# A fused chunk attention and wave MLP on one core: the written-out order of steps is replaced by another

## The chip, the core and the metric

The kernel runs on one core of a Trainium2 chip. The core has a matrix engine (PE, TensorE; its weight loads are listed apart as PEld), a vector engine (DVE), a scalar engine (ACT), GpSimd (POOL), and a sync engine (SP) that only issues transfers. Each engine executes its own list of instructions in order, and waits at an instruction for what another engine or a transfer has to bring. The metric is device time in microseconds (us); below, all times without a unit are us.

## The reference

Eight batches of 576 tokens with 8 heads of 64. Attention is local to chunks of 64 tokens; its output x (576 x 512 per batch) goes through a "wave" mixer over tokens and a channel mixer:

```python
scores = scale * np.matmul(q_c, k_c.transpose(0, 1, 2, 4, 3))   # 9 chunks of 64 x 64 per head
attn = np.exp(scores) / sum
out = np.matmul(attn, v_c)                                      # = x
theta = x @ w_theta
zr, zi = x * np.cos(theta), x * np.sin(theta)
y = np.einsum('ts,bsd->btd', w_tok_r, zr) + np.einsum('ts,bsd->btd', w_tok_i, zi)
u = x + y
return u + np.maximum(u @ w_ch, 0.0)
```

## The kernel before

Batches go in pairs p = 0 to 3. The 1152 tokens of a pair are nine row tiles of 128 (j = 0 to 8): tiles 0 to 3 of the first batch, 4 to 7 of the second, and tile 8 (M) with the last 64 tokens of both. Attention works on five groups of a pair: A (tiles 0, 1), B (2, 3), C (4, 5), D (6, 7) and M (8). Tensors are fp16 in SBUF, sums fp32 in PSUM, whose eight banks and all SBUF buffers are handed out by hand.

The whole program is a table, `ORDER`, of some 610 steps. Its order is the order in which each engine gets its instructions; no scheduler moves them. A step reads `kind.at.slot`: `S.0B.2` is the kind S on pair 0, group B, with bank 2. Numbers after `at` are banks or buffers; so a new order also hands out banks and buffers anew. An instruction that reuses one waits for its last reader.

The kinds, in the order in which a group passes them:

- `qk` loads q and k of a group (POOL's queue), `v` its v, `lw` a row tile of the two token matrices (`lw.03` is tile 3), `lp` w_theta, `lc` w_ch. `qk0.0A` and `qk1.0A` are the first two loads: heads 0 to 3 and 4 to 7 of group 0A, in fp32 by SP and ACT; `cy0` and `cv1` cast them on ACT and DVE.
- `T` (or `Tq`, `Tk`, `T0`, `T1`) transposes q and k in 32 x 32 blocks on DVE; `S` the score products on PE; `E` the exp on ACT; `V0`, `V1` the products with v for four heads each; `N0`, `N1` the division by the sum (a reciprocal and a product on DVE), which writes x.
- `X` turns x on PE, and `xa`, `xv` copy it out by ACT or DVE; `xd` does both by a transposing DMA from SP. `H` is the product with w_theta (four products of 512 columns a tile), `G` cos and sin on ACT, `Z` the two products on DVE that give zr and zi.
- `TW` turns a token tile (ten PE transposes), `twv` or `twa` copies it out by DVE or ACT. `Y` (or `Ya`, `Yb`, `Ym` for the shares of A, B and M, or of C, D and M) is the token product of an output tile, `A` the addition to x on DVE. For most of pairs 2 and 3 the token product is done on 2 x 2 blocks with fewer products: `sw`, `za`, `zb`, `zm` are the sums on DVE, `K` the products, `B` the additions.
- `U` turns u with `ua` or `uv` as copies, `ud` by DMA; `W` is the product with w_ch, `R` relu and addition on DVE, `st`, `sa`, `sg` the store, issued by SP, ACT or POOL.
- `dm.n.b` issues n products of zeros of full width into bank b. They serve no output.

ACT holds one table of functions at a time, exp or cos and sin; `table` loads the other when a step needs it.

Of the kernel before, what the change touches and what calls it, by code (L numbers as in the profile page):

```python
# [11 lines left out]
AF = mybir.ActivationFunctionType  # L12
ALU = mybir.AluOpType
# [5 lines left out]
Tk.0B v.0M v.0B Tq.0M.5 lw.03.2 S.0B.2 T1.0A E0.0A.0 V0.0A.0 Tk.0M S1.0A.4 E1.0A S.0M.6 lp.00 E.0M.1  # L19
V0.0M.7 N0.0A V1.0M.6 qk.0C.4 N1.0M V1.0A.4 dm.2.0 E.0B.2 lw.01.5 V1.0B.2 V0.0B.0 N1.0A X.0A.4  # L20
qk.1M.1 lw.02.3 N1.0B N0.0B xa.0A.1 X.0B.5 TW.03.3 v.0C N0.0M X.0M.7 xv.0B.2 H1.0A.5 G1.0A.0 H1.0B.0
G1.0B.3 xv.0M.4 Tq.0C.2 Z1.0A H0.0A.7 qk.0D.0 lw.00.6 G0.0A.1 v.0D twv.03 Z0.0A H.0M.5 H0.0B.4
G.0M.4 TW.01.6 G0.0B.1 Ya.03.3 Tk.0C S.0C.0 Z1.0B twv.01 v.1M E.0C.3 Z0.0B Ya.01.6 Yb.01 TW.02.4
twa.02 Z.0M Ym.01 T.1M.2 A.01 Yb.03 V0.0C.0 Ym.03 V1.0C.4 Tq.0D.1 S.1M.6 E.1M.4 Ya.02.7 Yb.02 Ym.02
N1.0C Tk.0D S.0D.4 N0.0C A.03 TW.00.0 qk.1B.2 A.02 X.0C.3 lw.04.0 E.0D.3 U.01.6 ua.01.0 U.02.4
ua.02.1 U.03.5 twv.00 Ya.00.0 V1.0D.6 uv.03.2 qk.1A.6 xv.0C.1 N1.0D V0.0D.4 H.0C.2 G.0C.1 qk.1D.3
V0.1M.6 N0.0D X.0D.4 xv.0D.3 v.1B N0.1M Z.0C Yb.00 v.1A Ym.00 v.1D H.0D.4 Ya.05.2 T.1B.4 G.0D.5
V1.1M.3 A.00 Ya.06.6 TW.04.0 S.1B.4 Ya.04.7 N1.1M X.1M.3 E.1B.4 Z.0D Yb.06 T.1A.4 Ym.06 S.1A.4
qk.1C.6 A.06 Yb.05 T.1D.5 xv.1M.3 U.06.6 twv.04 E.1A.1 Ym.05 Ya.07.4 V1.1B.0 qk.2M.3 A.05 ua.06.3
N1.1B V0.1B.5 N0.1B Yb.04 lc.00 S.1D.2 v.1C V1.1A.0 Yb.07 qk.2C.5 Ym.07 qk.2D.4 N1.1A E.1D.2 V0.1D.2  # L30
N0.1D X.1B.0 xa.1B.4 V1.1D.5 Ym.04 H.1M.1 H.1B.2 qk.2B.0 N1.1D V0.1A.5 A.07 qk.2A.2 qk.3B.1 Y.08.4
T.1C.7 A.04 N0.1A X.1A.5 U.04.6 G.1M.2 Z.1M xv.1A.1 U.00.7 S.1C.0 v.2M G.1B.6 E.1C.4 A.08 X.1D.5
xv.1D.2 v.2B W.06.2 R.06.3 U.07.0 H.1A.4 uv.04.3 V0.1C.2 v.3D uv.07.4 v.2A uv.00.5 W.00.7 G.1A.7
N0.1C U.05.0 U.08.6 uv.08.5 v.2C V1.1C.2 W.01.1 uv.05.6 H.1D.4 N1.1C X.1C.2 Z.1A Z.1B R.01.2 qk.3A.6
# [23 lines left out]
B4.30 K4.31 st.30 B4.31 K7.31 B7.31 W.36.1 R.36.5 U.35.5 uv.35.5 R1.31 sa0.31 W.38.0 R.38.4 W.26.2
R.26.10 sg.26 W.22.1 sa.36 R.22.12 W.35.5 ud.32.3 U.33.3 R.35.3 uv.33.9 ud.34.1 st1.31 W.32.6 st.38
sa.22 R.32.7 sg.32 st.35 W.37.4 R.37.9 sa.37 W.34.7 R.34.0 sg.34 W.33.0 dm.2.2 R.33.1 sa.33  # L60
""".split()


# [1 line left out]
def kernel(  # L65
# [11 lines left out]
    nc = tc.nc  # L77
    B, H, S, D = q.shape
# [11 lines left out]
    HH = H // 2  # L90
    scale = 1.0 / math.sqrt(D)
# [191 lines left out]
    def size(g):  # L283
        return 1 if g == "M" else 2
# [7 lines left out]
    def qk_t(which):  # L292
        def step(p, g, slot=None):
            n = CH if g == "M" else P
            if which != "k":
                st["T", p, g] = big(slot).rearrange(
                    "p (w h l s e) -> p w h l s e", w=2, h=H, l=32, s=2
                )
            a, z = {"q": (0, 1), "k": (1, 2), "qk": (0, 2)}[which]
            turn(  # L300
                st["T", p, g][0:n, a:z].rearrange("p w h l s e -> p (w h l s e)"),
                st["qk", p, g][0:n, a:z].rearrange("p w h s d -> p (w h s d)"),
            )

        return step
# [90 lines left out]

        return products

    def norm(f):
        def divide(p, g):  # L400
            n = size(g)
            j0 = GROUPS[g][0]
            ps = st.pop(("ps_x", p, g, f))
            recip = tmp.tile([P, 2, HH, 1], FP32, name="recip")
            nc.vector.reciprocal(out=recip[:, 0:n], in_=ps[:, :, :, D : D + 1])
            x = st["x", p][:, j0 : j0 + n, f * DM // 2 : (f + 1) * DM // 2]
            nc.vector.tensor_tensor(  # L407
                out=x.rearrange("p r (h d) -> p r h d", h=HH),
                in0=ps[:, :, :, 0:D],
                in1=recip[:, 0:n].broadcast_to((P, n, HH, D)),  # L410
                op=ALU.mult,
            )

        return divide
# [212 lines left out]
    def add_block(n):  # L627
        def add(p, i):
            x = st["x", p][:, [0, 2, 6, 4, 0, 6, 2][n - 1] + i]
            nc.vector.tensor_tensor(  # L630
                out=x, in0=st["ps_b", p, "ccccdff"[n - 1], i], in1=x, op=ALU.add
            )

        return add

    def u_t(p, j, b):
        ps = banks(b, 1, FP16)[:, 0:DM].rearrange("p (a c) -> p a c", c=P)
        for a in range(NDB):
            nc.tensor.transpose(ps[:, a, :], st["x", p][:, j, a * P : a * P + P], id16)  # L639
        st["ps_uT", p, j] = ps  # L640
# [119 lines left out]
    def store_half(queue, f):  # L760
# [78 lines left out]
```

## Time and profile before

| | us |
|---|---|
| median of 3 runs | 189.95 (189.6 to 190.64) |
| profiled execution | 190.72 |
| its span, first to last instruction | 189.0 |
| PE busy | 172.7 of the span (91%) |
| DVE busy | 157.8 (84%) |
| ACT busy | 83.6 (44%) |
| POOL busy | 88.9 (47%) |

The span is what the timeline shows; the time of an execution is some 1.7 longer. In rows of the timeline, the first number is the start from the beginning of the span, the second the duration, then engine, line, operation, out<-in and the number of instructions merged; in brackets the idle time before and what ended it. In rows of groups, the numbers behind the bar are the busy time in us and the mean of one in ns, then the idle time before them. Rows of DMA issues end with the time from issue to landing. A table of stretches has one row for each stretch, with the busy time of each engine in it.

### The profile page before, as it was taken

The numbers are of one execution on the slowest core, as the hardware profiler recorded it, in microseconds if no ns is written. First come the engines' busy times: TensorE is split into PE (matmuls) and PEld (weight loads), VectorE is DVE, ScalarE is ACT, GpSimd is POOL, SyncE is SP. The second block draws the span as 40 slices with busy tenths as digits, with TensorE's granted clock in tenths as the row PEclk, the third lists the DMA queues.
The fourth block names the chain that finished last, engine by engine and source line by source line (L and its number), as shares of the span: only waits on it lengthen the run. The fifth ranks groups of instructions, "written<-read, shape, count | busy, mean of one in ns | idle before, by whom it ended". The sixth has DMA issues, their size and how long they took to land.

```text
span 189.0 us, 5983 instructions
## 1 busy us (share of the span) xinstructions
PE 172.7 (91%) x2574; PEld 91.4 (48%) x2574; DVE 157.8 (84%) x289; ACT 83.6 (44%) x103; POOL 88.9 (47%) x126
## 2 busy tenths in 40 slices
PE   0068899999999999999999999999999999999991
PEld 0056645564555555454546545555544444445440
DVE  0564659978898988798879999999999999999981
ACT  3114588275836983663104969823272740000000
POOL 8999279689579783489968600000000010011021
PEclk9999999999999999999999999999999999999999
DMA  5999999999999999999999997899766822597985
GB/s 154 206 157 169 189 146 147 152 168 182 158 135 153 169 180 182 170 100 109 164 169 101 166 131 108 248 257 197 155 186 134 87 83 44 140 306 206 197 278 224
DMA packets 100586, 31.21 MB, mean 165 GB/s; under 512 B 91984, under 2 KB 96464, under 8 KB 100560
## 3 DMA queue, kind: packets, MB, share of 16 engines
q0 software_dynamic: 76128, 17.59, 98.7%
q1 hardware_dynamic: 21328, 9.18, 23.6%
q10 hardware_dynamic: 3104, 4.06, 6.8%
q8 instruction: 20, 0.33, 0.7%
q14 instruction: 6, 0.05, 0.1%
HBM read 33.06 MB, written 9.44 MB: 225 GB/s over the span
## 4 chain that ended last, share of the span: by engine, by line
PE 87%; POOL 4%; DVE 3%; DMA 2%; ACT 1%; issue 0%; ACTq 0%; DVEq 0%; POOLq 0%
PE psum L529 21%; PE psum L657 16%; PE psum L450 16%; PE psum L619 15%; PE psum L326 6%; PE psum L390 5%; PE psum L422 4%; DMA v<-in_v_dram 2%; PE psum L265 2%; PE psum L639 2%; POOL big L175 1%; POOL big L180 1%; DVE x L407 1%; POOL v L234 1%; ACT mid L473 1%; PE psum L164 1%
## 5 line engine op out<-in xcount | busy, mean ns | idle before, releaser
L234 POOL DMA_DIRECT2D v<-in_v_dram x54 | 41.1, 794 | 9.6 <-DMA big<-in_k_dram 5.9
L756 POOL DMA_DIRECT2D out_dram<-mid x6 | 3.3, 552 | 74.7 <-ACT big L473 45.1
L529 PE MATMUL psum<-zr,wT 128*128 128x512 f16 (+1 forms) x108 | 35.0, 382 | 0.1
L657 PE MATMUL psum<-wch,uT 128*128 128x512 f16 x140 | 34.5, 379 | 0.0
L450 PE MATMUL psum<-wtheta,mid 128*128 128x512 f16 x144 | 34.3, 386 | 0.0
L529 PE MATMUL psum<-zi,wT 128*128 128x512 f16 (+1 forms) x108 | 33.3, 379 | 0.0
L356 ACT ACTIVATE mid<-psum 128x1024 f16<-128x1024 f32 (+1 forms) x19 | 17.4, 930 | 32.9 <-PE psum L326 32.2
L407 DVE TENSOR_TENSOR x<-psum,recip 128x512 f16<-128x512 f32 (+1 forms) x40 | 25.5, 638 | 1.4
L662 DVE SCALAR_TENSOR_TENSOR mid<-psum,x 128x512 f32<-128x512 f32 (+1 forms) x37 | 24.4, 669 | 1.7 <-PE psum L657 1.5
L287 DVE STREAM_TRANSPOSE big<-big 128x1024 f32<-128x1024 f32 (+3 forms) x25 | 24.9, 1013 | 0.2
L529 PEld LDWEIGHTS <-wT 128*128 128x128 f16 (+1 forms) x216 | 16.5, 102 | 16.8 <-issue 0.4
L326 PE MATMUL psum<-big 32*64 32x64 f16 x1152 | 15.1, 199 | 9.6 <-DVE big L287 9.6
L450 PEld LDWEIGHTS <-mid 128*128 128x128 f16 x144 | 14.1, 100 | 16.4 <-issue 1.1
L472 ACT ACTIVATE big<-psum,pihalf 128x1024 f16<-128x1024 f32 x14 | 15.6, 1115 | 10.9 <-PE psum L450 10.9
L326 PEld LDWEIGHTS <-big 32*64 32x64 f16 x1152 | 12.9, 112 | 15.1 <-DVE big L287 10.1
L657 PEld LDWEIGHTS <-uT 128*128 128x128 f16 x140 | 13.0, 98 | 13.9
L630 DVE TENSOR_TENSOR x<-psum,x 128x512 f16<-128x512 f32 x28 | 18.6, 684 | 0.4 <-PE psum L619 0.2
L153 ACT ACT_TABLE_LOAD x12 | 15.4, 1283 | 3.9 <-DMA out_dram<-mid 2.4
L551 DVE TENSOR_TENSOR x<-psum,x 128x512 f16<-128x512 f32 x20 | 13.4, 679 | 3.4 <-PE psum L529 3.4
L180 POOL DMA_DIRECT2D big<-in_q_dram x15 | 13.9, 926 | 3.6 <-PE psum L326 1.8
L473 ACT ACTIVATE big<-psum 128x1024 f16<-128x1024 f32 x14 | 14.3, 1021 | 0.0
L180 POOL DMA_DIRECT2D big<-in_k_dram x15 | 13.8, 920 | 0.2 <-DMA v<-in_v_dram 0.2
(66 smaller groups left out, 210.9 us busy)
## 6 DMA issues: line engine op xcount, KB each, us to landing
big<-in_q_dram POOLq DMA_DIRECT2D x15, 256.0 KB, 6.4
big<-in_k_dram POOLq DMA_DIRECT2D x15, 256.0 KB, 7.0
out_dram<-mid SPq DMA_DIRECT2D x14, 256.0 KB, 3.0
out_dram<-mid ACTq DMA_DIRECT2D x11, 256.0 KB, 2.6
v<-in_v_dram POOLq DMA_DIRECT2D x18, 128.0 KB, 5.8
v<-in_v_dram POOLq DMA_DIRECT2D x36, 64.0 KB, 5.6
out_dram<-mid POOLq DMA_DIRECT2D x6, 256.0 KB, 2.8
out_dram<-mid SPq DMA_DIRECT2D x5, 128.0 KB, 3.7
```

Of the source, the lines that this page charges most:

```text
L180: nc.gpsimd.dma_start(t[:, w].rearrange("p h s d -> p h (s d)"), ap[2 * p + bb, :, s0 : s0 + GT, :].rearrange("h (p s) d -> p h (s d)", s=2),)
L234: nc.gpsimd.dma_start(v16[rows, slot + t, :, 0:D], v[b, :, t0 : t0 + m, :].rearrange("h s d -> s h d"),)
L287: nc.vector.transpose(out.bitcast(FP32).rearrange("p (x l s) -> p x s l", l=32, s=2), in_.bitcast(FP32).rearrange("p (x s d) -> p x s d", ...
L326: nc.tensor.matmul(ps[half[to], r, h], t[quarter[c], 1, h, :, e], t[quarter[c], 0, h, :, e], start=(e == 0), stop=(e == 1), tile_position= ...
L356: nc.scalar.activation(out=eT[:, 0:n].rearrange("p r h i -> p (r h i)"), in_=st.pop(("ps_s", p, g)).rearrange("p r h i -> p (r h i)"), fun ...
L407: nc.vector.tensor_tensor(out=x.rearrange("p r (h d) -> p r h d", h=HH), in0=ps[:, :, :, 0:D], in1=recip[:, 0:n].broadcast_to((P, n, HH, D ...
L450: nc.tensor.matmul(ps, xT[:, a, :], wtheta16[:, a, :], start=(a == 0), stop=(a == NDB - 1))
L529: nc.tensor.matmul(ps[half[b]] if j == MID else ps, w, z[:, cols], start=(kt == 0), stop=(kt == 2 * KT),)
L619: nc.tensor.matmul(ps, lhs, rhs, start=(k == 0 and n in (1, 5, 6)), stop=(k == len(pieces) - 1), skip_group_check=(n in (2, 3, 4, 7)),)
L630: nc.vector.tensor_tensor(out=x, in0=st["ps_b", p, "ccccdff"[n - 1], i], in1=x, op=ALU.add)
L657: nc.tensor.matmul(ps, uT[:, a, :], wch16[:, a, :], start=(a == 0), stop=(a == NDB - 1))
L662: nc.vector.scalar_tensor_tensor(out=out, in0=ps, scalar=0.0, in1=x, op0=ALU.max, op1=ALU.add)
```

## The change

The `ORDER` table is replaced from the third load on: a new sequence of the same work, with new banks and buffers. The first rows of both:

```diff
-on.00 init.00 qk1.0A.0 pre.00 qk0.0A.1 qk.0B.2 cy0.0A.3 cv1.0A qk.0M.4 T0.0A.1 S0.0A.0 Tq.0B.0 v.0A
+on.00 init.00 qk1.0A.0 pre.00 qk0.0A.1 cv1.0A.2 T1.0A.11 dm.4.5 qk.0B.3 S1.0A.0 E1.0A.0 dm.2.1
```

In numbers of steps, what differs between the tables:

| kind | before | after |
|---|---|---|
| products of zeros (`dm`) ahead of the first theta product / between it and the last W / behind | 2 / 0 / 2 | 18 / 1 / 4 |
| x turned on PE (`X`) / by DMA (`xd`) | 14 / 6 | 13 / 7 |
| its copies by ACT / DVE | 7 / 7 | 5 / 8 |
| token tiles copied by DVE / ACT | 4 / 1 | 0 / 5 |
| u turned on PE (`U`) / by DMA (`ud`) | 13 / 22 | 12 / 23 |
| its copies by DVE / ACT | 8 / 5 | 5 / 7 |
| stores by SP / ACT / POOL | 16 / 13 / 6 | 17 / 3 / 15 |

(The halves of tile 31, which both tables turn and store in two parts, are not counted.) All other kinds have as many steps as before, with the same sizes.

In the code, a `Tk` step no longer makes a new view of its buffer unless it is given one, which lets `Tq` and `Tk` stand in either order; the rest adds kinds that no step of the new table uses.

```diff
     def qk_t(which):
         def step(p, g, slot=None):
             n = CH if g == "M" else P
-            if which != "k":
+            if slot is not None:
...
-    def norm(f):
+    def norm(f, scalar=False):
...
+            if scalar:
...
+                        nc.scalar.activation(
+                            out=x[:, r, h], in_=ps[:, r, h, 0:D], func=AF.Copy,
+                            scale=recip[:, r, h],
+                        )
...
+    def copy_block(n):
...
+    def add_run(n):
...
+        "n0": norm(0, True), "n1": norm(1, True),
```

Behind the table, line numbers are one higher in the new file, and higher still behind the new functions.

Three places. The first is the beginning of DVE's and of ACT's lists. On DVE, `CAST` rows are the casts of group 0A, `STREAM_TRANSPOSE` rows of 128x8x2x32 a half of A, or q or k of B, and those of 64x8x2x32 q or k of M. Before:

```order
L212 CAST big<-big 128x512 x3
L287 STREAM_TRANSPOSE big<-big 128x8x2x32 x3
L287 STREAM_TRANSPOSE big<-big 64x8x2x32
L287 STREAM_TRANSPOSE big<-big 128x8x2x32
L287 STREAM_TRANSPOSE big<-big 64x8x2x32
L405 RECIPROCAL recip<-psum 128x8
```

Now:

```order
L213 CAST big<-big 128x512 x2
L288 STREAM_TRANSPOSE big<-big 128x8x2x32 x2
L213 CAST big<-big 128x512
L288 STREAM_TRANSPOSE big<-big 128x8x2x32 x2
L288 STREAM_TRANSPOSE big<-big 64x8x2x32 x2
L406 RECIPROCAL recip<-psum 128x8
```

The half of A that is loaded first is cast and transposed first, and q of B before the other half; all transposes of A, B and M come before the first division.

The second is ACT's list around the first cos and sin pairs (`ACTIVATE` with pihalf is cos, the one behind it sin; 128x9x128 is the copy of a token tile). Before:

```order
L442 COPY mid<-psum 128x1024
L153 ACT_TABLE_LOAD
L153 ACTIVATE first<-pihalf 128x1
L472 ACTIVATE mid<-psum,pihalf 128x512
L473 ACTIVATE mid<-psum 128x512
```

Now:

```order
L452 COPY mid<-psum 128x1024
L278 COPY wT<-psum 128x9x128
L154 ACT_TABLE_LOAD
L154 ACTIVATE first<-pihalf 128x1
L482 ACTIVATE mid<-psum,pihalf 128x512
L483 ACTIVATE mid<-psum 128x512
```

The copy of token tile 3 has come to ACT, ahead of the pairs; that of tile 1 stands behind the third of the five pairs.

The third is POOL's queue of loads, first around w_theta. 32x8x128 is q or k of M, 128x8x128 q or k of another group; 128x576 is a part of a token tile. Before (the tiles 3, then w_theta, C of pair 0, tile 1, M of pair 1, tile 2, v of C):

```order
L247 DMA wtheta_69<-in_moe_w_theta_dram 128x4x512
L180 DMA big<-in_q_dram 128x8x128
L180 DMA big<-in_k_dram 128x8x128
L244 DMA big<-in_moe_w_tok_r_dram 128x576
L244 DMA big<-in_moe_w_tok_i_dram 128x576
L175 DMA big<-in_q_dram 32x8x128 x2
L175 DMA big<-in_k_dram 32x8x128 x2
```

Now:

```order
L248 DMA wtheta_69<-in_moe_w_theta_dram 128x4x512
L176 DMA big<-in_q_dram 32x8x128 x2
L176 DMA big<-in_k_dram 32x8x128 x2
L245 DMA big<-in_moe_w_tok_r_dram 128x576
L245 DMA big<-in_moe_w_tok_i_dram 128x576
L181 DMA big<-in_q_dram 128x8x128
L181 DMA big<-in_k_dram 128x8x128
```

Token tile 3 stands ahead of w_theta in both. Behind it the same three loads follow in the reverse order; tile 0, which was loaded behind D, now comes fourth. And around w_ch, before (C of pair 1, M of pair 2, w_ch, v of C of pair 1):

```order
L180 DMA big<-in_q_dram 128x8x128
L180 DMA big<-in_k_dram 128x8x128
L175 DMA big<-in_q_dram 32x8x128 x2
L175 DMA big<-in_k_dram 32x8x128 x2
L250 DMA wch_70<-in_moe_w_ch_dram 128x4x512
L234 DMA v_72<-in_v_dram 128x8x64
L234 DMA v_72<-in_v_dram 64x8x64 x2
```

Now (w_ch, M of pair 2, C of pair 1, B of pair 2, v of C of pair 1):

```order
L251 DMA wch_70<-in_moe_w_ch_dram 128x4x512
L176 DMA big<-in_q_dram 32x8x128 x2
L176 DMA big<-in_k_dram 32x8x128 x2
L181 DMA big<-in_q_dram 128x8x128
L181 DMA big<-in_k_dram 128x8x128
L181 DMA big<-in_q_dram 128x8x128
L181 DMA big<-in_k_dram 128x8x128
L235 DMA v_72<-in_v_dram 128x8x64
L235 DMA v_72<-in_v_dram 64x8x64 x2
```

w_ch has moved ahead of two groups, and B of pair 2 ahead of the v of C.

More of the change, by code (lines that the diff above doesn't have):

```diff
@@ L23 @@
[L23 to L34, printed above, removed]
@@ L58 @@
[L58 to L60 removed]
+on.00 init.00 qk1.0A.0 pre.00 qk0.0A.1 cv1.0A.2 T1.0A.11 dm.4.5 qk.0B.3 S1.0A.0 E1.0A.0 dm.2.1
+Tq.0B.4 qk.0M.5 dm.1.3 cy0.0A v.0B T0.0A S0.0A.6 dm.2.2 Tk.0B v.0M S.0B.4 dm.4.1 Tq.0M.6 Tk.0M
+E.0B.1 V0.0B.2 N0.0B V1.0B.4 dm.4.0 S.0M.3 v.0A E.0M.2 E0.0A N1.0B V1.0M.1 V0.0A.4 N1.0M V0.0M.2
@@ new lines @@
+Y.08.4 V0.1D.6 V0.1A.2 A.08 N0.1A H.1B.0 lc.00 W.01.3 W.00.5 X.1A.4 W.02.2 N0.1D qk.2M.4 T.2M.7
+X.1D.6 qk.1C.8 G.1B.3 U.08.7 qk.2B.9 T.1C.11 S.1C.0 E.1C.3 xv.1A.6 S.2M.4 R.00.9 xv.1D.1 sw.01.5
+H.1A.5 v.1C R.01.11 E.2M.10 R.02.2 U.06.0 V0.1C.3 uv.08.2 ua.06.6 sw.02.7 V1.1C.1 N0.1C qk.2A.6
+W.08.7 T.2B.10 W.03.0 W.04.3 N1.1C G.1A.1 qk.3M.0 W.06.4 Z.1A Z.1B X.1C.1 xa.1C.13 H.1D.5 R.06.12
+G.1D.12 qk.2C.5 Z.1M v.2A R.08.4 H.1C.1 T.2A.13 Y.11.4 A.11 v.2B G.1C.14 Z.1C v.2M Y.13.5 S.2A.6
+S.2B.1 Z.1D v.2D qk.2D.18 E.2A.0 v.3M Y.10.4 E.2B.6 V0.2B.6 V1.2B.1 R.04.3 R.03.1 T.2C.15 Y.17.3
@@ new lines @@
+N1.2B V1.2A.0 N0.2B V0.2M.7 A.10 N1.2A V1.2M.2 Y.18.6 V0.2A.0 A.17 N0.2M U.07.4 A.18 uv.07.7 Y.15.3
+W.07.7 N0.2A v.3B N1.2M T.2D.2 X.2B.1 xv.2B.13 A.13 Y.16.2 R.07.8 S.2D.4 S.2C.0 Y.14.6 U.13.7
+T.3M.16 E.2D.6 A.16 A.15 X.2M.4 E.2C.10 v.3D v.2C A.14 V0.2D.2 N0.2D V1.2D.0 ua.13.8 W.05.5 N1.2D
+qk.3A.3 T.3A.1 U.15.6 ua.15.9 R.05.0 Y.12.7 V1.2C.2 N1.2C V0.2C.0 xa.2M.6 N0.2C A.12 v.3A H.2M.6
+G.2M.10 H.2B.4 xd.2D.6 X.2C.1 Z.2M qk.3D.17 T.3D.4 W.15.2 S.3A.6 xa.2C.13 qk.3C.8 T.3C.18 ud.12.1
+xd.2A.10 G.2B.11 H.2C.0 H.2D.3 W.12.5 Z.2B st.03 R.15.13 st.05 st.02 G.2C.17 H.2A.0 ud.11.0 Z.2C
@@ new lines @@
+sg.16 B5.21 K4.21 sg.07 B4.21 za.23 V1.3C.3 G.3D.5 V1.3M.2 V0.3C.5 N1.3M W.14.1 R.14.10 N1.3C N0.3C
+W.20.7 st.00 za.24.2 K6.20.2 B6.20 K6.21.1 B6.21 sg.17 Z.3D xd.3B.0 xd.3A.8 H.3A.3 G.3A.0 H.3B.5
+ud.21.1 zb.24 K7.20 xd.3M.2 Z.3A K7.21 G.3B.15 ud.28.0 B7.20 zb.33.3 xd.3C.12 B4.20 Z.3B H.3C.3
+W.21.0 st.14 K1.30.5 G.3C.1 B7.21 H.3M.2 R.21.13 W.28.6 Z.3C za.31.8 R.28.9 ud.26.8 G.3M.0 Z.3M
+ud.22.2 W.26.3 ud.25.5 sg.12 R.20.1 ud.27.9 B1.30 za.32.11 W.22.1 W.25.0 ud.24.6 W.24.4 R.24.11
+ud.23.4 K1.31.6 B1.31 Y.38.2 W.27.7 zb.31 zb.32 sg.20 R.26.8 K2.31 R.25.10 A.38 ud.38.7 K5.30.4
@@ new lines @@
+B5.30 za.33 K2.30 B2.30 zb.34.17 W.23.3 K5.31.0 B2.31 R.27.12 st.21 ud.30.3 K3.30 R.23.2 B3.30
+zm.30.5 K3.31 sg.10 K6.30.2 R.22.0 B6.30 K6.31.4 B3.31 sg.24 B6.31 za.34 K4.30 B4.30 W.38.7 K4.31
+B5.31 sa.26 B4.31 ud.36.1 R.38.1 W.30.3 R.30.6 U1.31.1 K7.31 B7.31 W.36.0 K7.30 B7.30 U0.31.7
+ud.37.0 ud.34.8 uv0.31.2 sa.38 W.37.6 sg.27 sg.28 uv1.31 sg.23 U.32.5 R.36.11 Wp.31.3.4 W0.31
+R0.31.7 R.37.8 ud.35.6 W.35.2 R.35.13 ud.33.9 W1.31 st.30 ua.32.4 sg.25 sg.36 sg.37 W.34.7 R.34.5
+st.22 W.32.0 R1.31 st1.31 R.32.12 st.32 W.33.1 R.33.4 sa0.31 sa.35 dm.2.5 st.33 sg.34 dm.2.7
@@ L406, in divide @@
             x = st["x", p][:, j0 : j0 + n, f * DM // 2 : (f + 1) * DM // 2]
+            x = x.rearrange("p r (h d) -> p r h d", h=HH)
+            if scalar:
+                for r in range(n):
+                    for h in range(HH):
+                        nc.scalar.activation(
+                            out=x[:, r, h], in_=ps[:, r, h, 0:D], func=AF.Copy,
+                            scale=recip[:, r, h],
+                        )
+                return
             nc.vector.tensor_tensor(
-                out=x.rearrange("p r (h d) -> p r h d", h=HH),
+                out=x,
                 in0=ps[:, :, :, 0:D],
@@ L634, in add_block, with copy, add @@
         return add
+    def copy_block(n):
+        def copy(p, i, slot=None):
+            if slot is not None:
+                st["run", p, n] = mid(slot).rearrange("p (i d) -> p i d", i=2)
+            nc.scalar.copy(out=st["run", p, n][:, i], in_=st["ps_b", p, "c", i])
+        return copy
+    def add_run(n):
+        def add(p, _):
+            j = [0, 2, 6][n - 1]
+            x = st["x", p][:, j : j + 2]
+            nc.vector.tensor_tensor(out=x, in0=st["run", p, n], in1=x, op=ALU.add)
+        return add
     def u_t(p, j, b):
@@ L795 @@
         work.update({f"K{n}": block(n), f"B{n}": add_block(n)})
+        if n < 4:
+            work.update({f"C{n}": copy_block(n), f"D{n}": add_run(n)})
     work.update({
+        "n0": norm(0, True), "n1": norm(1, True),
         "sw": sum_w, "zm": sum_mid,
```

44 lines of the change are left out of this document (17 added, 27 removed).

## The prediction

> **What bounds the kernel now.** I read the page's first line, then the table of stretches, then the timeline of the stretch in which the table shows PE idle.
>
> ```profile
> span 189.0 us, 5983 instructions
> ...
> core 0: us, PE busy (x) PEld busy (x) DVE busy (x) ACT busy (x) POOL busy (x), PEclk, DMA share, GB/s
> 0.00:10.00 10.00, 0.64 (x32) 0.51 (x32) 3.27 (x7) 2.42 (x4) 9.38 (x18) 1.00 1.14 180
> 10.00:20.00 10.00, 7.38 (x218) 5.72 (x218) 5.99 (x15) 2.72 (x5) 8.56 (x13) 1.00 1.76 165
> 20.00:24.20 4.20, 4.08 (x26) 2.76 (x27) 2.31 (x6) 2.16 (x3) 1.14 (x2) 1.00 1.61 189
> 24.20:40.00 15.80, 15.70 (x287) 9.04 (x286) 13.18 (x26) 10.99 (x17) 13.08 (x19) 1.00 1.58 148
> 40.00:100.00 60.00, 60.00 (x1052) 31.41 (x1052) 50.96 (x92) 32.65 (x39) 46.62 (x61) 1.00 1.83 157
> 100.00:180.00 80.00, 80.00 (x940) 39.74 (x937) 77.62 (x140) 32.62 (x38) 8.51 (x12) 1.00 0.86 163
> ```
>
> From 40 to 180 PE has no gap at all (60.00 of 60, 80.00 of 80). So the time is: when PE comes into its dense stretch, plus the products still left on its list, plus the tail. A new order can win only by an earlier start, a shorter list, or smaller holes before 40; it loses wherever it opens a hole behind 40. DVE is the engine to watch: 77.62 of 80 from 100 on.
>
> ```profile
> 10.20 1.07 PE L326 MATMUL psum<-big 32*64 32x64 f16 x64 [0.58 <-DVE big L287]
> ...
> 13.11 0.83 POOL L247 DMA_DIRECT2D wtheta<-in_moe_w_theta_dram  x1
> ...
> 17.52 1.09 PE L390 MATMUL psum<-v,mid 64*64 64x65 f16 x32
> 18.54 1.03 PE L422 MATMUL psum<-id,x 128*128 128x128 f16 x8
> ...
> 20.94 1.31 PE L265 MATMUL psum<-id,big 128*128 128x128 f16 x10
> 21.49 0.58 POOL L175 DMA_DIRECT2D big<-in_k_dram  x1 [2.77 <-DMA wtheta<-in_moe_w_theta_dram]
> 22.18 0.61 PE L422 MATMUL psum<-id,x 128*128 128x128 f16 x4
> 22.58 5.28 PE L450 MATMUL psum<-wtheta,mid 128*128 128x512 f16 x20
> ...
> 23.43 0.15 PEld L450 LDWEIGHTS <-mid 128*128 128x128 f16 x1 [0.28 <-issue]
> 23.86 0.15 PEld L450 LDWEIGHTS <-mid 128*128 128x128 f16 x1 [0.28 <-issue]
> 24.24 3.12 PEld L450 LDWEIGHTS <-mid 128*128 128x128 f16 x15 [0.23 <-issue]
> ```
>
> ```profile
> wtheta<-in_moe_w_theta_dram POOLq DMA_DIRECT2D x1, 512.0 KB, 8.1
> ```
>
> Theta's weights, issued at 13.11, land 8.1 later, at 21.2; POOL's next issue, which waited for that landing, starts at 21.49. The first theta product runs only at 22.58, since the transposes at 18.54 to 22.18 stand ahead of it on PE. And PE runs at half clock until then, although the granted clock reads 1.00: the weight loads of the first theta products are 0.43 apart (23.43, 23.86), while 15 of them take 3.12 from 24.24 on, 0.208 each. The transposes are as slow: 8 take 1.03 at 18.54, and 0.45 later (first row of the next fence).
>
> **The change, part by part.** *Work behind the first theta product.* In both orders the same steps stand ahead of theta: all scores and attention products of A, B and M of pair 0, their three transposes, and token tile 3. So the list behind it differs only by what the table of counts says: one x tile (2A) goes through a transposing DMA instead of eight PE transposes, one u tile fewer goes through PE, and one product of zeros (0.22) stands behind theta.
>
> ```profile
> 104.85 0.45 PE psum L422 x8
> ...
> 177.15 0.22 PE psum L639 x4
> ...
> 184.34 0.59 PE L164 MATMUL psum<-zeros 128*128 128x512 f16 x2
> 184.54 0.69 DVE L662 SCALAR_TENSOR_TENSOR mid<-psum,x 128x512 f32<-128x512 f32 x1 [0.17 <-PE psum L657]
> ```
>
> That is -0.45 - 0.22 + 0.22 = -0.45. The four zero products at the end stand behind the last real product, and nobody waits for them: 0. Before, the real list ran from 22.58 to 184.34, 161.8; the last add follows to 185.2, and the stores to 189.0. This tail of 4.7 keeps its form (last add, then one store), and I leave it alone.
>
> *Start of theta.* Its load stands at the same place in POOL's queue, behind the same bytes, so it lands at 21.2 again. The work ahead of it must be done by then. The new order casts and transposes the first half of A alone (DVE is free of the second half's wait), and the zeros stand in PE's waits. Scores of B, at 10.20 before, now stand behind the second half's transposes and two more zeros (0.43 each): about 11.4. Then come four zeros, V of B, four zeros and the scores of M, to about 17.6 at half clock, or 15.5 if the clock rises by 14; then two exps of 0.6 (row below), V of A and M, and the transposes. At full clock from 14 on, the last transpose ends at 20.3, one microsecond ahead of theta; with the clock rising only at 17, theta starts at 22.1. I take a start at 21.3, 1.3 earlier than 22.58: -1.3. Range: 21.3 to 22.1.
>
> *The clock at theta.* The first tile of four products took 1.66 (22.58 to 24.24), and takes 4 x 0.216 = 0.86 at full clock: -0.8 if the zeros have raised it, 0 if not. I take -0.8, because 18 full-width products stand ahead of theta where before there were two.
>
> [...]
>
> *ACT and the holes up to 40.*
>
> ```profile
> 24.44 0.69 ACT L472 ACTIVATE mid<-psum,pihalf 128x512 f16<-128x512 f32 x1 [2.25 <-PE psum L450]
> ...
> 25.50 0.69 ACT L472 ACTIVATE mid<-psum,pihalf 128x512 f16<-128x512 f32 x1
> ...
> 29.90 1.28 ACT L153 ACT_TABLE_LOAD   x1
> ```
>
> The five cos and sin pairs go at 1.06 each (24.44 to 25.50) and end at 29.9. Now the first starts at about 22.35, but the copy of token tile 1 (1.12, below) stands among them: 5 x 1.06 + 1.1 gives 28.8. So ACT is only 1.1 ahead, not 2.1. Its next customer is Yb.01, which needs the last pair, and PE gets there at about 30; so no hole from that. The hole that does open is at S.0C. Its k is now the last of the three loads behind theta, whose sum of bytes is as before:
>
> ```profile
> big<-in_k_dram POOLq DMA_DIRECT2D x1, 64.0 KB, 5.6
> ```
>
> That is the last of the three before, issued at 21.49, landed at 27.1. So k of C lands at 27.1, its transpose (0.69, next fence) ends at 27.9 to 28.7, as DVE has the phase products of A in front of it; PE, with 20 theta products, token tile 1, S.1M, one zero and Ya.03 behind 21.3, is there at 27.6. A hole of 0.3 to 1.1. Before, PE lost 1.0 in its holes between 27.7 and 40 (12.3 of time for 11.3 of work at full-clock spacings). New against old: -0.7 to +0.4, taken as 0.
>
> *DVE.*
>
> ```profile
> L287 DVE STREAM_TRANSPOSE big<-big 128x512 f32<-128x512 f32 x8 | 5.4, 688 | 0.0
> L440 DVE COPY mid<-psum 128x1024 f16<-128x1024 f16 x5 | 3.4, 690 | 1.6 <-PE psum L422 1.5
> L649 DVE COPY uT<-psum 128x512 f16<-128x512 f16 x8 | 3.1, 418 | 1.0 <-PE psum L639 1.0
> L275 DVE COPY wT<-psum 128x1152 f16<-128x1152 f16 x3 | 2.3, 752 | 0.4 <-PE psum L265 0.4
> L275 DVE COPY wT<-psum 128x576 f16<-128x576 f16 x1 | 0.4, 440 | 0.0
> L356 ACT ACTIVATE mid<-psum 128x512 f16<-128x512 f32 x4 | 2.4, 592 | 5.6 <-PE psum L326 5.6
> L277 ACT COPY wT<-psum 128x1152 f16<-128x1152 f16 x1 | 1.1, 1119 | 0.5 <-PE psum L265 0.5
> ```
>
> Four token copies go to ACT (3 x 0.75 + 0.44 = 2.7 off DVE), three u copies leave (1.25) and one x copy comes (0.69): DVE loses 3.3. It was idle 9.0 from 40 to 100 and 2.4 from 100 to 180. To end 2.5 earlier in the same dense way it has to find 2.5 and is given 3.3, most of it before 55. So PE stays fed: 0. ACT gets at most 4 x 1.12 = 4.5 more where it was idle 27.35 of 60 and 47.38 of 80: hidden, except for the one copy above.
>
> *Queues.* Nine more stores go out by POOL and ten fewer by ACT. POOL was busy 8.51 of 80 from 100 on, so they are hidden there; the last add's store leaves by SP. The loads of pair 1's C now stand behind w_ch and behind 2B:
>
> ```profile
> 14.73 0.97 POOL L180 DMA_DIRECT2D big<-in_k_dram  x1
> ...
> big<-in_k_dram POOLq DMA_DIRECT2D x1, 256.0 KB, 9.4
> ...
> 57.37 2.28 POOL L234 DMA_DIRECT2D v<-in_v_dram  x3
> ...
> v<-in_v_dram POOLq DMA_DIRECT2D x1, 64.0 KB, 7.0
> ...
> 69.71 0.32 PE L390 MATMUL psum<-v,mid 64*64 64x65 f16 x16
> ```
>
> The last part of v.1C, issued at 58.9, landed 7.0 later at 65.9 and was first used at 69.71. With 2B's pair ahead it lands 2.9 later, at 68.8: that is what C's pair took behind theta, from 21.2 to 14.73 + 9.4 = 24.1. PE gets to it at about 70, by the products ahead of it in the new list. A margin of 1.2: 0 cost, but the thinnest cover behind 40.
>
> **Sum.** -0.45 - 1.3 - 0.8 + 0 = -2.55, rounded to -2.5, so a span of 186.5. The profiled execution took 190.72 for its span of 189.0; the median of the runs, 189.95, lies 0.8 below it. On the median: 187.5. Ends: if the holes shrink by 0.7, 186.8; with theta at 22.1, the clock at half for its first tile and 0.4 more holes, 189.5.
>
> **Rivals.** *The clock comes late or falls back.* Between 17.5 and 21.3 PE has nearly only transposes. Before, a stretch with PE 7.38 of 10 busy on small products and transposes did not raise the clock. If theta starts at half clock and gets it back as before, 1.66 in, the cost is 0.8 to 1.6: 188.3 to 189.1. [...]
>
> *Slower: the zeros stand in the way.* If they do not raise the clock before theta, they cost what they take on PE. From S.0B at 11.4, at the half-clock rows: 1.07 + eight zeros at 0.43 (3.4) + two V steps and S.M (1.1 + 0.7) end at 17.6; two exps to 19; V of A and M (1.4); X.B (1.03), a zero (0.43), token tile 3 (1.31), X.A and X.M (1.5). Theta would start at 24.6, 2.0 later than before, still at half clock. Less the 0.45 off the list and what the load-bound hole at S.0C swallows (0.3 to 0.7): 190.8 to 191.5. It decides if full clock is not there by about 19.
>
> *No gain: given back behind 40.* DVE, or v.1C, sets the pace. If v.1C lands 3 later than I work out, PE waits 1.8 there; if DVE's 3.3 come too early to be of use at 100 to 180, where only 2.4 were idle, the end follows DVE. Then 189.0 to 190.3. Against it: 9.0 of idle DVE from 40 to 100, into which work can move.
>
> **How the numbers follow.** This kernel's runs lie within 0.5%, so under 189.0 is faster and over 190.9 slower. Forecast (186.4 to 188.6): 0.54. Late clock (188.3 to 189.5): 0.17, two thirds of it under 189.0. No gain: 0.15, mostly same. Zeros in the way: 0.11. Else 0.03. Faster: 0.54 + 0.11 + 0.03 = 0.68; same 0.18; slower 0.14. The range takes the forecast's whole spread and reaches into the last two: 186.2 to 190.4.
>
> **What would show it.** Right: the first theta product at 21.3 to 22, its weight loads 0.21 apart from the first on; PE 60.00 of 60 from 40 to 100 and DVE no busier than 77 of 80 behind that; PE's last product near 181.8. Wrong: theta products 0.43 apart, a V step of 1C that waits for v, or PE gaps behind 60 that end on DVE.

## The result: slower by 1.2%

| | before | changed |
|---|---|---|
| median | 189.82 (7 runs, 189.32 to 190.7) | 191.8 (7 runs, 191.19 to 194.35) |
| ratio | | 1.0119 [1.0085, 1.0153] |
| profiled execution | 190.72 | 191.19 |
| its span | 189.0 | 189.4 |

Beside the kernel before on another chip, twelve more runs of the changed kernel gave 191.86 against 190.2, a ratio of 1.0084 [1.0053, 1.0115]. The forecast was 187.5. In all ratios, runs that took over 1.5% more than the fastest of their kernel are left out; medians keep them.

The two profiled executions lie only 0.5 apart, since the one before is the slowest of its seven and the one after the fastest; the medians are 2.0 apart. So the profile below shows the least of what the change costs.

The profile after, first by the table of stretches:

```profile
span 189.4 us, 5965 instructions
...
core 0: us, PE busy (x) PEld busy (x) DVE busy (x) ACT busy (x) POOL busy (x), PEclk, DMA share, GB/s
...
10.00:20.00 10.00, 9.14 (x227) 5.30 (x228) 4.62 (x11) 2.23 (x4) 8.19 (x13) 1.00 1.76 168
20.00:40.00 20.00, 19.17 (x333) 10.90 (x335) 16.15 (x36) 16.56 (x24) 17.36 (x24) 1.00 1.74 172
40.00:100.00 60.00, 60.00 (x1119) 33.14 (x1122) 52.99 (x93) 34.45 (x42) 48.10 (x64) 1.00 1.76 148
100.00:110.00 10.00, 10.00 (x177) 5.22 (x177) 9.75 (x18) 7.06 (x10) 3.14 (x5) 1.00 1.87 189
110.00:130.00 20.00, 16.70 (x318) 8.10 (x317) 16.23 (x28) 11.35 (x13) 1.92 (x4) 1.00 0.87 201
130.00:180.00 50.00, 50.00 (x357) 22.96 (x355) 46.78 (x86) 11.24 (x13) 4.56 (x9) 1.00 0.65 150
```

Up to 110 this is the forecast: 60.00 of 60, no hole. Then PE idles 3.3 of 20, and afterwards none again. Before, PE was busy 20.00 of these 20:

```profile
110.00:130.00 20.00, 20.00 (x373) 10.13 (x372) 19.66 (x35) 13.05 (x15) 0.00 (x0) 1.00 0.88 197
```

The head came as foretold, too, by the timeline:

```profile
15.28 1.38 PE L165 MATMUL psum<-zeros 128*128 128x512 f16 x4
...
22.01 3.62 PE L460 MATMUL psum<-wtheta,mid 128*128 128x512 f16 x16
...
21.95 2.96 PEld L460 LDWEIGHTS <-mid 128*128 128x128 f16 x15
...
182.08 2.75 PE L683 MATMUL psum<-wch,uT 128*128 128x512 f16 x12
184.67 1.03 PE L165 MATMUL psum<-zeros 128*128 128x512 f16 x4
```

Four zeros from 12.45 on took 1.89, these four 1.38: the clock rose among them, at 16.0 by the trace's record of the granted clock, against 24.2 before (the rise is the record's first entry; for what lies ahead of it the table reads 1.00). Theta starts at 22.01, and its weight loads are 0.20 apart from the first on (2.96 for 15). The zeros behind the last real product start at 184.67, before at 184.34. Without the 3.3 of holes, if all behind them had moved up, that would be 181.4; the prediction named 181.8. So a gain was there, and more than all of it went in one stretch. This is PE in that stretch, and who waited for what:

```profile
108.46 1.90 PE L460 MATMUL psum<-wtheta,mid 128*128 128x512 f16 x8
112.11 1.90 PE L460 MATMUL psum<-wtheta,mid 128*128 128x512 f16 x8 [1.76 <-DMA mid<-x]
113.85 1.03 PE L683 MATMUL psum<-wch,uT 128*128 128x512 f16 x4
114.72 1.89 PE L460 MATMUL psum<-wtheta,mid 128*128 128x512 f16 x8
117.65 1.90 PE L683 MATMUL psum<-wch,uT 128*128 128x512 f16 x8 [1.04 <-DMA uT<-x]
...
123.61 1.90 PE L683 MATMUL psum<-wch,uT 128*128 128x512 f16 x8 [0.51 <-DMA uT<-x]
```

H.2D (the row at 112.11) waits for its transposing DMA `xd.2D`, W.11 (117.65) and W.16 (123.61) for `ud.11` and `ud.16`: 1.76 + 1.04 + 0.51 = 3.3. These are transfers that SP issues. Its queue after:

```profile
104.93 1.58 SPq L444 DMA_TRANSPOSE mid<-x  x1
106.57 1.87 SPq L673 DMA_TRANSPOSE uT<-x  x1
108.53 2.85 SPq L444 DMA_TRANSPOSE mid<-x  x1
111.43 1.53 SPq L782 DMA_DIRECT2D out_dram<-mid  x3
113.00 3.59 SPq L673 DMA_TRANSPOSE uT<-x  x2
```

and before:

```profile
110.85 1.40 SPq L434 DMA_TRANSPOSE mid<-x  x1
112.30 4.88 SPq L647 DMA_TRANSPOSE uT<-x  x3
```

The DMA part of the profile gives the time from issue to landing. Of the changed kernel, for the issues at 104.93 and at 101.64 (the last load, k of 3B), and of the kernel before, for that at 110.85:

```profile
mid<-x SPq DMA_TRANSPOSE x1, 7.1
big<-in_k_dram POOLq DMA_DIRECT2D x1, 256.0 KB, 9.1
```

```profile
mid<-x SPq DMA_TRANSPOSE x1, 3.7
```

The first transposing DMA came 5.9 earlier than before, and took 7.1 instead of 3.7. Before, the last six loads left POOL like this (timeline), and the last two of them, of 64 KB, took (DMA rows):

```profile
102.69 4.51 POOL L234 DMA_DIRECT2D v<-in_v_dram  x6
```

```profile
v<-in_v_dram POOLq DMA_DIRECT2D x2, 64.0 KB, 5.4
```

They had landed by 111.6, just after SP began. Now the last load lands at 101.64 + 9.1 = 110.7, in the middle of SP's transposes. The packets of the queues (number, MB, share) show what the tile waits for; q0 is POOL's queue, q1 that of SP. Of the changed kernel, from 104.9 to 108.5 and from 108.5 to 110:

```profile
q0 software_dynamic: 2948, 0.63, 197.1%
...
q0 software_dynamic: 310, 0.26, 76.1%
q1 hardware_dynamic: 431, 0.11, 64.3%
```

The DMA issued at 104.93 moves nothing before 108.5; the first packet of SP's queue runs at 108.9, 4.0 after the issue. Before, the first one ran 1.7 after the issue at 110.85.

### The profile page after: what moved, and what is told of

Read it like the earlier page. It is cut to its first block, busy times and chain, and to the rows that moved or that the text cites. A ratio compares the mean times of both kernels' runs of the same rounds, so it can differ in the third digit from the quotient of the medians.

```text
span 189.4 us, 5965 instructions
## 1 busy us (share of the span) xinstructions
PE 174.8 (92%) x2581; PEld 89.9 (47%) x2581; DVE 155.3 (82%) x283; ACT 86.1 (45%) x107; POOL 94.2 (50%) x136
## 4 chain that ended last, share of the span: by engine, by line
PE 75%; DVE 6%; DMA 5%; SPq 5%; ACT 4%; issue 2%; POOL 1%; DVEq 0%; POOLq 0%
PE psum L539 20%; PE psum L629 14%; PE psum L683 14%; PE psum L460 10%; PE psum L327 5%; PE psum L391 4%; DVE big L288 3%; DMA big<-in_q_dram 3%; PE psum L165 3%; DMA uT<-x 2%; PE psum L432 2%; SPq L673 2%; PE psum L665 1%; PE psum L266 1%; SPq L782 1%
## 5 line engine op out<-in xcount | busy, mean ns | idle before, releaser
L782 POOL DMA_DIRECT2D out_dram<-mid x14 | 7.6, 547 | 73.4 <-DVE mid L688 72.0
L460 PE MATMUL psum<-wtheta,mid 128*128 128x512 f16 x144 | 33.8, 380 | 1.8 <-DMA mid<-x 1.8
L683 PE MATMUL psum<-wch,uT 128*128 128x512 f16 x140 | 33.9, 380 | 1.5 <-DMA uT<-x 1.5
L357 ACT ACTIVATE mid<-psum 128x1024 f16<-128x1024 f32 (+1 forms) x19 | 16.9, 932 | 31.4 <-PE psum L327 25.3
L460 PEld LDWEIGHTS <-mid 128*128 128x128 f16 x144 | 13.3, 98 | 17.2 <-DMA mid<-x 2.2
L327 PEld LDWEIGHTS <-big 32*64 32x64 f16 x1152 | 12.4, 111 | 10.0 <-DVE big L288 6.1
L327 PE MATMUL psum<-big 32*64 32x64 f16 x1152 | 14.2, 198 | 2.8 <-DVE big L288 2.4
L677 ACT COPY uT<-psum 128x512 f16<-128x512 f16 x7 | 4.1, 585 | 27.7 <-DMA uT<-x 23.9
```

The costliest lines, as they stand in the source:

```text
L327: nc.tensor.matmul(ps[half[to], r, h], t[quarter[c], 1, h, :, e], t[quarter[c], 0, h, :, e], start=(e == 0), stop=(e == 1), tile_position= ...
L357: nc.scalar.activation(out=eT[:, 0:n].rearrange("p r h i -> p (r h i)"), in_=st.pop(("ps_s", p, g)).rearrange("p r h i -> p (r h i)"), fun ...
L460: nc.tensor.matmul(ps, xT[:, a, :], wtheta16[:, a, :], start=(a == 0), stop=(a == NDB - 1))
L683: nc.tensor.matmul(ps, uT[:, a, :], wch16[:, a, :], start=(a == 0), stop=(a == NDB - 1))
```

## The experiments

Three explanations were put against each other. A: a transposing DMA that is issued while loads are on their way lands only behind them, so PE waits. B: SP's own queue is too long, and the issue comes too late. C: the clock of the new head costs the time.

**2D turned on PE.** Eight PE transposes and a copy by DVE in place of one transposing DMA.

```diff
-xd.2D.6 X.2C.1 Z.2M
+X.2C.1 X.2D.3 Z.2M xv.2D.6
```

> The changed kernel, with x of 2D turned on PE (eight transposes, copied by DVE) instead of by the transposing DMA. Theory A (transposing DMAs that are issued while the last loads are still on the DMA engines land 5 to 7 us after issue, and PE waits for them): the 1.8 us wait of H.2D goes, SP starts on ud.12 about 1.6 earlier, so the waits of W.11 (1.0) and W.16 (0.5) shrink; 0.46 of PE comes on top. PE's last W ends 1.5 to 3 earlier than 184.7, the time is 188.5 to 190.2. Rival B (SP's queue is simply too long, whatever the loads do): H.2D's wait goes, those of W.11 and W.16 stay, 190 to 190.6. Rival C (the new head costs the time, by its clock): no change from the changed kernel.

188.54, a ratio of 0.9881 [0.9837, 0.9924] that rests on three runs; a second time, with twelve runs:

> 2D alone turned on PE, once more, as the measure for the two others: in ratio to the kernel before 0.984 to 0.992, mean clock 1.00 in every run.

189.65, 0.9968 [0.9935, 1.0001], a little outside of what was expected. Both lie below the changed kernel, by 1.2 to 2.4%. One step, taken off the transposing DMAs, brings back all that was lost; that it brings more, only the three runs of the first show. In the profile of the first, H.2A still waits 0.85 for `xd.2A` and W.11 0.28; in that of the second H.2A does not, but W.11 waits 0.79 and W.16 0.84. The head is the same in all of these, and theta's first sixteen products, at full clock, take 3.61 in the second of them, as against 3.62 in the changed kernel, so C is not the cause.

**Two u transposes issued earlier.**

```diff
-... Z.2M ... ud.12.1 xd.2A.10 ... ud.11.0 Z.2C ud.17.2
+A.18 ud.11.0 ud.17.2 ... ud.12.1 xd.2D.6 ... xd.2A.10
```

> The changed kernel, with the transposes of u 11 and 17 moved up in SP's queue to about 92 us, and u 12 ahead of x 2D. Theory A: they land late too (5 us or more after issue, loads being in flight), but in time; W.11's wait (1.0) goes, H.2D's wait (1.8) stays or grows by up to 1.9, as u 12 now goes ahead of it. Time 190 to 192. Rival B: all transposes come forward, both waits go, 188.5 to 189.5.

195.15 in the median (193.87 to 195.69, and one run of 228.26), a ratio of 1.0217 [1.0158, 1.0275]: worse. The waits of W.11 and W.16 are gone, but `xd.2D` stands behind `ud.12` now, is issued at 107.38 and lands at 113.80:

```profile
113.85 3.60 PE L460 MATMUL psum<-wtheta,mid 128*128 128x512 f16 x8 [3.66 <-DMA mid<-x]
```

The eight products behind that wait take 3.60 instead of 1.90: the clock fell to half at 113.0 and came back at 119.8 (more below).

**The last loads left out.** q and k of 3B and v of 3C are not loaded, and the transposes of 3B read q and k of 3C, so this kernel computes something else in these two groups. SP's steps are as in the changed kernel.

```diff
-v.3C
-qk.3B.9
```

> The changed kernel without its last loads: q and k of 3B (the transposes of 3B read the tile of 3C instead) and v of 3C are not loaded. The work of all engines but POOL's five issues stays. Theory A: x 2D is issued at about 105 as before and lands 3.5 to 4.5 later instead of 7.1, so H.2D (due at 110.2) does not wait, u 12, x 2A and u 11 come earlier as well, and 2.5 to 3.5 of the lost time come back: 188 to 189.3. Rival B: x 2D lands at 112 again and nothing changes (191.2 to 192).

189.0, a ratio of 0.9934 [0.9895, 0.9974]. `xd.2D`, issued at 104.09, takes

```profile
mid<-x SPq DMA_TRANSPOSE x1, 3.1
```

instead of 7.1, and H.2D follows the product before it without a gap. 768 KB of loads taken away make the same DMA 4.0 faster: that is A, for the 1.76 at H.2D. The holes at W.11 and W.16 stay:

```profile
114.29 1.90 PE L685 MATMUL psum<-wch,uT 128*128 128x512 f16 x8 [0.44 <-DMA uT<-x]
...
120.86 1.90 PE L685 MATMUL psum<-wch,uT 128*128 128x512 f16 x8 [1.01 <-DMA uT<-x]
```

That is 1.45, against 1.04 + 0.51 = 1.55 with the loads, so the last loads do not explain these two. Here `ud.11` is issued at 111.19 and lands 3.1 later, as PE stands waiting: for W.11 in this run it is B, the late issue.

**2D's transposing DMA issued earlier.** A store of 03 is moved up so that its buffer is free for 2D. R.12 takes buffer 6 in its place, which R.11 and R.10 write again before tile 12 is stored; so this kernel's output for tile 12 is that of another tile, with the same number of steps.

```diff
+R.03.1 st.03
+N1.2D xd.2D.1
-xd.2D.6
-st.03
-R.12.1
+R.12.6
```

> The changed kernel, with the store of row tile 03 moved up to just behind its relu, and x 2D transposed into the buffer that this frees, as soon as x is there (issue at about 102 instead of 105; R.12 takes the other buffer). Theory A: issued into the same traffic it lands 6 to 7 after issue, 108 to 109, just ahead of H.2D; the 1.8 wait goes, and the transposes behind it on SP come about 2.5 earlier, so W.11's wait goes too: 188.5 to 189.7. Rival B (SP's transposes land a fixed 3.6 after issue, and only the late issue for want of a buffer costs): x 2D lands by 106, same gain in time; the trace tells them apart.

191.61, 1.0055 [1.0017, 1.0092]. Its DMA rows, for the issues at 100.74 (k of 3B) and at 101.53 (`xd.2D`):

```profile
big<-in_k_dram POOLq DMA_DIRECT2D x1, 256.0 KB, 10.8
mid<-x SPq DMA_TRANSPOSE x1, 10.7
```

This is the sharpest test between A and B. SP issues 3.4 earlier than in the changed kernel, and the tile lands at 101.53 + 10.7 = 112.2, at the same time as there (104.93 + 7.1 = 112.0), and 0.7 behind the load of k (111.5). An issue 3.4 earlier brings the landing forward by nothing; B falls for this tile. PE waits longer than in the changed kernel, as it comes to the tile earlier, and the products behind the wait are slow (half clock from 113.3 to 116.7):

```profile
112.27 2.64 PE L460 MATMUL psum<-wtheta,mid 128*128 128x512 f16 x8 [2.52 <-DMA mid<-x]
```

**The last loads held back.** One store is moved from SP to POOL, ahead of the last loads. All work is done; PE, DVE and ACT have the same lists as in the changed kernel.

```diff
-st.15
+R.15.13 sg.15
```

> The changed kernel with one store (15) moved from SP to POOL, ahead of the last loads (q and k of 3B, v of 3C): these leave only when W.15 is added, at about 108.5 instead of 100 to 102. Same PE list, same DVE and ACT lists, same loads. Theory A (a transposing DMA lands only when the loads issued before it have landed): the transposing DMA of 2D lands at 107 to 108 instead of 112.07, H.2D does not wait, and the time is 189 to 190; what is left are the transposes of u.11, u.17, u.16, which then meet the held loads. Theory B (SP's own queue is too long): SP's queue is one store shorter, nothing else changes, 191 to 192.

201.14, a ratio of 1.0586 [1.0521, 1.0651]. The time missed the expectation by 11, the mechanism did not. `xd.2D`, issued at 104.53, took 3.4, and H.2D did not wait:

```profile
mid<-x SPq DMA_TRANSPOSE x1, 3.4
```

What I had wrong was when POOL would be released. The store waits for DVE, which came to R.15 only at 110.9, and POOL went on at 112.18; the loads left from 112.74 to 116.8 and met the next transposes on SP:

```profile
112.18 0.58 POOL L782 DMA_DIRECT2D out_dram<-mid  x1 [13.85 <-DVE zr L509]
112.74 2.28 POOL L235 DMA_DIRECT2D v<-in_v_dram  x3
114.97 0.93 POOL L181 DMA_DIRECT2D big<-in_q_dram  x1
115.84 0.94 POOL L181 DMA_DIRECT2D big<-in_k_dram  x1
...
127.25 0.26 PE L327 MATMUL psum<-big 32*64 32x64 f16 x2 [9.80 <-DVE big L288]
```

```profile
big<-in_k_dram POOLq DMA_DIRECT2D x1, 256.0 KB, 10.1
...
uT<-x SPq DMA_TRANSPOSE x2, 9.4
```

The first fence is the timeline, the second the DMA rows of the issues from 115.5 to 119.5. So the one kernel shows both sides: with hardly a load on its way the DMA of 2D takes 3.4, its first packet 1.3 after the issue, and two that were issued behind loads (`ud.16` and `ud.18`) take 9.4 in the middle. The k of 3B landed at 125.9, its transposes on DVE had waited for it, and PE stood 9.8 ahead of the scores of 3B; the clock fell to half in this wait as well, from 120.9 to 131.1.

**Zeros in the wait.** Products of zeros fill PE's wait ahead of H.2D, eight in the changed kernel, fourteen in the one with the u transposes moved up.

```diff
-H.2D.3
+dm.8.3 H.2D.3        (the other: dm.14.3 H.2D.3)
```

> The changed kernel with eight more products of zeros, 1.7 us, ahead of theta's products of 2D, where PE waits 1.76 for the transposing DMA of 2D. If the runs of the changed kernel with a mean clock of 0.979 to 0.991 lost it in this wait: the clock stays at 1.00 in every run and the times draw together at 191.2 to 191.7, against up to 194.35 without the zeros. If the clock is lost elsewhere (between the first zeros and theta): the same spread as without them, some runs at 0.98 to 0.99 and over 192.5. If the zeros come in the way of the products of 2D: 1 to 1.7 slower than 191.5 in every run.

> The order with the transposes of u.11 and u.17 moved up, where PE waited 3.66 for 2D and then ran at half clock from 113.0 to 119.8, with fourteen products of zeros, 3.0 us, ahead of theta's products of 2D. If the wait drops the clock: the clock stays at 1.00, the products of 2D are 0.216 apart from the first, and the time is 192 to 192.5 instead of 195.15, since half clock from 113.85 to 119.8 cost 3.0. If the clock fell for another reason: again 0.98 and 195.

The second: 193.29 (192.69 to 193.44, and one run of 615.74), 1.0161 [1.0101, 1.0222], against 195.15 and 1.0217 without the zeros; mean clocks 0.996 to 0.998 instead of 0.981 and 0.982. By the two ratios, work that does nothing took about 1.1 off the time, less than the 3.0 expected, and their intervals overlap. In the profile, the products behind the wait run at full clock:

```profile
114.90 1.90 PE L460 MATMUL psum<-wtheta,mid 128*128 128x512 f16 x8 [1.17 <-DMA mid<-x]
```

The first: 192.19, 1.0068 [1.0026, 1.011], not to be told from the changed kernel itself; the runs (apart from one of 980.56) still spread from 189.9 to 193.3, mostly at a clock of 0.996 and more. So the spread of the changed kernel's times is not the clock alone. The changed kernel once more:

> The changed kernel once more, beside the others on the same chip. 191 to 192, in ratio to the kernel before 1.005 to 1.015; mean clock 1.00 in some runs and 0.98 to 0.99 in others, the latter 1 to 3 slower. If the wait for 2D drops the clock, the runs with the lower clock are those in which the wait was long, and the profile of such a run shows half clock from 113 on.

In its runs, 191.86 in the median, the mean clock was below 0.992 in 3 of 12, and these took 191.98, 193.72 and 193.9; in the first seven it was 4, with 191.8 to 194.35. The profiled run here was one with a clock of 1.00 and a wait of 2.56 at H.2D, so the expectation that a profile would show where the clock fell was not met for this kernel. With 1.03 and 0.31 at W.11 and W.16, its holes come to 3.9, against 3.3 in the first profile. Among the changed kernel and its variants the lower clock (below 0.992) came in orders where H.2D or another product waits in this stretch: in all 4 runs of the order with u moved up, 5 of 10 with 2D issued early, 2 of 12 with eight zeros (the profiled one waits 0.71), all with the loads held; in none of 4 with u moved up and fourteen zeros; and in none of the 59 runs of the kernels that turn 2D on PE or leave the last loads out. Of 74 runs of the kernel before beside these, 2 had it (193.47 and 259.64), for a reason that no trace here shows.

**The head without zeros.** The order with 2D on PE, without the 18 zeros ahead of theta (the text below counts 20).

```diff
-dm.4.5  dm.2.1  dm.1.3  dm.2.2  dm.4.1  dm.4.0  dm.1.3
```

> The order with 2D turned on PE, without the 20 products of zeros that stand ahead of the first theta product. My sum (0.8 for the first theta tile at full clock, and the part of the 1.3 that is owed to transposes at full clock): the clock rises only behind the first theta products, at 22 to 25, and the time is 0.8 to 1.6 above the one with the zeros, 189.3 to 190.2. If the zeros stand in the way as much as they help: 188.0 to 189.0, no difference. If the clock rises early without them: up to 0.5 faster.

189.74, a ratio of 0.9994 [0.9963, 1.0026], against 0.9881 and 0.9968 with the zeros. The weight loads of theta's first products are 0.42 apart (22.06 and 22.48), the clock rises at 22.5, and theta starts at 21.63, against 21.69 with the zeros (the second profile with 2D on PE) and 22.01 in the changed kernel:

```profile
21.63 4.07 PE L460 MATMUL psum<-wtheta,mid 128*128 128x512 f16 x16
...
22.06 0.15 PEld L460 LDWEIGHTS <-mid 128*128 128x128 f16 x1 [0.28 <-issue]
22.48 2.51 PEld L460 LDWEIGHTS <-mid 128*128 128x128 f16 x12 [0.28 <-issue]
```

So the zeros are not seen to bring theta forward; they bring sixteen products from 4.07 to 3.62, 0.45 in this execution. In the times their gain lies between 0.3% and 1.1%, by which of the two measures it is taken from, and only the larger is clear of the intervals.

**2D and 2A on PE, and then u ahead of the stores.** S.3A and W.15 change places, too.

```diff
-xd.2D.6 X.2C.1 Z.2M            W.15.2 S.3A.6     xd.2A.10
+X.2C.1 X.2D.3 X.2A.2 Z.2M xv.2D.6 xv.2A.10 ... S.3A.6 W.15.2
```

> Both 2D and 2A turned on PE, so that no transposing DMA of an x tile is left in this stretch. With only 2D on PE, H.2A still waited 0.85 for its transposing DMA (issued at 106.81, landed at 113.17) and W.11 0.28. Theory A: H.2A's wait goes, -0.85, for eight transposes more on PE, +0.45, and SP issues u.11 some 1.3 earlier, but still into the loads that land at 110 to 111: 0.3 to 0.7 below the order with 2D alone on PE. Theory B (SP's queue is too long): the same sign, but W.11 and W.16 no longer wait at all. If DVE, which gets 0.7 more to copy, is in the way: no gain, or up to 0.5 slower.

188.86, 0.9944 [0.9913, 0.9974]. No product waits for a transfer in this stretch. One wait is left, for DVE, which has one copy more than with 2D alone on PE:

```profile
109.04 1.02 PE L683 MATMUL psum<-wch,uT 128*128 128x512 f16 x4 [0.62 <-DVE mid L450]
...
182.26 1.03 PE L165 MATMUL psum<-zeros 128*128 128x512 f16 x4
```

> As the one with 2D and 2A on PE, and the transposes of u.11 and u.17 ahead of three stores on SP. Theory A: they are issued some 1.6 earlier, but land when the loads have landed, at 111 to 113 as before; W.11's wait goes if it was 0.3 or less: -0.3 to 0. Theory B: each is ready 1.6 earlier, W.11 has no wait, -0.3 or more. If the stores that now stand behind hold up the buffers of the sums: 0.3 slower.

189.12, 0.9931 [0.9903, 0.9958], the same within the intervals: with nobody waiting for them, an earlier issue of the u transposes shows no gain. Both are faster than the kernel before; against 2D alone on PE (0.9968) the intervals overlap. With two transposing DMAs fewer in SP's queue, W.11 and W.16 do not wait either, which fits B for these two; when only SP's queue was changed (u moved up), the two waits went as well, but PE came there later.

## Why the prediction was wrong, by its own steps

- *Queues, and no hole behind 40: 0.* This is the step that failed. The list is shorter by what the transposing DMA of 2A saves PE (0.45), but I did not ask what it and its neighbours cost on SP and among the loads: of SP I said only that the last add's store leaves by it. In place of the 0 the runs showed 3.3 of waits, in the stretch from 110 to 130. Of these, 1.76 is H.2D's: the new table issues that DMA 5.9 earlier than before, into the loads, where it takes 7.1. With the 3.7 that it took before, the tile would have been there at 108.6 (an estimate, 104.93 + 3.7), ahead of H.2D; at 7.1 it came at 112.07. SP's row of 110.85 beside the loads of before, which land up to 111.6, would have shown it. The other 1.55, at W.11 and W.16, is SP's queue rather than the last loads, as far as the runs tell.
- *Start of theta, -1.3.* 22.01, at the late end of the range given (21.3 to 22.1), with a clock that rose at 16.0, between the 14 and the 17 of its two cases: -0.6.
- *The clock at theta, -0.8.* Held: 0.20 between the weight loads from the first on, and half clock for the first ones without the zeros (0.45 in that execution).
- *Holes up to 40, DVE and v of 1C, 0 each.* PE is at 60.00 of 60 from 40 to 100 and never waits for v, nor for DVE from 40 to 110. DVE's busy time fell by 2.5 (157.8 to 155.3), where 3.3 were counted. Ahead of 40 it was not better than before: from 24.2 to 40, PE was busy 15.36 of 15.80, before 15.70. PE was 2.9 ahead of before by its end without the holes (184.3 against 181.4); list, theta and clock give 0.45 + 0.6 + 0.8 = 1.85, and no row shows where the rest of about 1 came from. So it is in part luck that 181.4 lies so near the 181.8 of the prediction: theta brought 0.7 less than the sum has, and about 1 came that is not in it.
- *Rivals.* "Given back behind 40" names the right place and two wrong causes, DVE and v.1C. "Falls back" came in a form that I had not thought of: not between the zeros and theta, but in the wait at H.2D, and in some runs only. "The zeros stand in the way" is refuted: theta starts at 22.01, not at 24.6.

## What to carry to other kernels

When a new order moves a transposing DMA, its price is not the landing time that it had before but when it is issued against the loads that are on their way: add what is left of those loads (here 7.1 in place of 3.7, and 10.7 when it was issued 3.4 earlier still). Where PE has the 0.45 and DVE the copy (0.69) to spare, a tile that is due in such a stretch is better turned on PE (here 0.9881 and 0.9968, against 1.0119 and 1.0084 with the transposing DMA). And a wait at a PE that has to be at full clock may cost the clock besides, in one execution and not in the next, as 2.52 did here and 2.56 did not, so its price can be more than its length.

## What the runs showed of the hardware

- The transposing DMA of 2D takes 3.1 to 3.7 with no more than the end of the loads on its way, and 7.1 to 10.7 behind loads that take some 9 to 11 themselves; issued at 101.53 or at 104.93, it lands at 112.2 or 112.1, 0.7 and 1.4 behind the last of them. Others, issued from 112 to 130 with no load on its way, took 2.5 to 4.9 in the profiles of the kernel before and the changed one.
- It is mainly the data that is late. With the last loads held back or left out, SP's first packet runs 1.3 after the issue, and before 1.7; in the changed kernel it runs 4.0 after it, and with 2D issued early SP's queue moves nothing in the first 2.0 (101.53 to 103.5). Once it moves, packets of both queues run in the same stretch: 310 of POOL's and 431 of SP's from 108.5 to 110 in the changed kernel. What holds the first one back no row here shows.
- Full clock was lost in PE's waits of 3.66 (half clock for 6.8), of 9.80 (10.2) and of 2.52 (3.4), and kept in those of 1.76 and 2.56. The length alone does not decide it, and what else does is not shown. The fall at 113.3 came 1.0 behind the end of the wait of 2.52 (109.75 to 112.27); behind that of 2.56 (110.40 to 112.96) there was none.
